# Queueing the vector pieces of the attention values ahead of the gate/value vector work of the next matmul group

## The chip, the cores and the metric

One NeuronCore of a Trainium2 chip. The metric is the device time of one execution in microseconds (us), the median over runs. Engines are named as in the profile: PE is TensorE's matmuls, PEld its weight loads, DVE is VectorE, ACT is ScalarE, POOL is GpSimd, SP is SyncE. L320 is line 320 of the kernel.

## The reference

Attention with a local window of 96 keys and 8 global keys, on 4 batches of 8 heads, 768 positions and head size 64, feeds a gated feed-forward block:

```python
scores = scale * q @ k.T + bias(head, distance); masked outside window and global keys
a = softmax(scores);  x = (a @ v) as [3072 tokens, 512]
out = (silu(x @ w_gate) * (x @ w_val)) @ w_out      # w: 512 x 1536, 1536 x 512
```

## The kernel before

It interleaves two streams by hand. One is the feed-forward stream: for each of 8 token blocks of 384 tokens and 12 slices of 128 hidden units a gate group, a value group and an output group of matmuls. The other is a list of attention steps (`tr` transposes, `sc` scores, `va` values), of which one is put in whenever enough matmul work has gone by. The order of calls is the order on each engine: in the trace of this kernel a transpose of `den` whose input was complete at 43.78 us starts at 45.88, after the `sl` of 45.41 that was called before it.

An attention value block leaves TensorE as a numerator `num` and a denominator `den` in two PSUM banks. Its vector work is not issued at once but appended to a list:

```python
            def invert():                       # PSUM den -> 1/den, one number per 32 columns
                nc.vector.transpose(dT[:, 0:n_q], den[:, 0:n_q])
                nc.vector.reciprocal(out=dR[:, 0:nb], in_=...dT...)

            def spread():                       # back to 128x384
                nc.vector.transpose(rb..., dR...)
                if not fast:
                    nc.gpsimd.tensor_mul(dst, ns[:, 0:n_q], rb[:, 0:n_q])   # L279, dst is in xT

            def scale_num():                    # batch 0 only
                nc.vector.tensor_mul(dst, num[:, 0:n_q], rb[:, 0:n_q])      # L282

            later.append(invert)
            later.append(spread)
            if fast:
                later.append(scale_num)
            else:
                nc.scalar.copy(out=ns[:, 0:n_q], in_=num[:, 0:n_q])
```

The gate and value groups:

```python
        products(t, f, which, c0, NC)                     # 4 matmuls into one of 3 or 4 rotating PSUM banks
        if which == 0:
            nc.scalar.activation(out=th, in_=dst, func=AF.Tanh, scale=0.5)
            nc.vector.scalar_tensor_tensor(out=sl, in0=th, ..., in1=dst, ...)   # L320, frees the bank
        else:
            nc.vector.tensor_mul(hTs[t][:, f, :], dst, gv["sl"])                # L324, frees the bank
```

The scores step multiplies the exponentials by a mask, on VectorE or on GpSimd (L234, L238): both inputs are in SBUF. And the loop:

```python
    for t, f, work, fn in groups:
        ...                              # loads of later batches; at f == 0 all pieces are popped
        fn()                             # a gate, value or output group
        run_later(1)                     # one pending piece
        owed += work * quota.get(t, 0.0)
        while owed >= 1.0 and todo:
            run_later(len(later))
            for step in todo[0][1].pop(0):
                step()
            ...
```

The loads that matter below are issued from GpSimd's queue in this order, ahead of the loop: `load_w(3)`, `load_wo(0)`, `load_wo(1)`, `load_wo(2)`, `load_qk(1, 2, 4)` (queries and keys of batch 1, heads 2 and 3), `load_v_rest(1, 0..3)`; `load_qk(1, 4, 8)` follows in the loop.

The softmax here doesn't subtract the row's maximum and nothing guards it: scores larger than these inputs give would overflow.

Of the kernel before, what the change touches and what calls it, by code (L numbers as in the profile page):

```python
# [37 lines left out]
def kernel(  # L38
# [137 lines left out]
    def run_later(n):  # L176
        for _ in range(n):
            if later:
                later.pop(0)()
# [291 lines left out]
    for t, f, work, fn in groups:  # L471
        if (t, f) not in seen:
            seen.add((t, f))
            for ld in loads.get(NFF * t + f, []):
                ld()
        if f == 0:
            run_later(len(later))
        if t == 1 and f == 0:
            state["x"] = ["x0", "x1", "x2"]
        fn()  # L480
        run_later(1)
        owed += work * quota.get(t, 0.0)
        while owed >= 1.0 and todo:
            run_later(len(later))
            for step in todo[0][1].pop(0):
                step()
            owed -= 1.0
            if not todo[0][1]:
                assert t <= todo[0][0]
                todo.pop(0)  # L490
                owed = 0.4
# [39 lines left out]
```

## Time and profile before

| | before |
|---|---|
| time, median of 4 runs | 270.75 us (270.39 to 271.23) |
| span in the profile | 268.5 us |
| TensorE busy | 247.8 us, 92% |
| VectorE busy | 181.3 us, 68%, 389 instructions |
| TensorE's waits after 43 us | 4.0 us in all |

How to read it: an engine's busy share says little by itself; TensorE's busy share is high nearly everywhere, so what VectorE does matters only where TensorE stops for it. The prediction below shows the lines: the stretches, TensorE's own waits, and the two places in the timeline where those waits lie.

All mask products of VectorE in the kernel before (durations are min/median/max in ns, then the time of the first and last start).

```profile
L238 DVE TENSOR_TENSOR at<-at,masks x52: 341/380/2980, 10.1 to 197.3; 128x432 f16<-128x432 f16 x52
```

The median is 380 ns, the longest 2980.

### The profile page before, as it was taken

How to read it: one execution, taken by the hardware profiler on the slowest of the kernel's cores; microseconds unless marked ns; L12 is line 12 of the kernel's file. 1: busy time of each engine (PE TensorE's matmuls, PEld its weight loads, DVE VectorE, ACT ScalarE, POOL GpSimd, SP SyncE). 2: the span in 40 equal slices, each digit the busy share in tenths (PEclk: the TensorE clock that was granted, in tenths of full speed). 3: DMA queues.
4: the chain of work that ended last, by engine and by line, in shares of the span. 5: the costliest groups of instructions: out<-in, count | busy, mean ns of one | idle time of the engine just before them, and what ended most of it. 6: DMA issues, size and time to landing. Idle time of an engine off the chain costs nothing.

```text
span 268.5 us, 5705 instructions
## 1 busy us (share of the span) xinstructions
PE 247.8 (92%) x2240; PEld 142.2 (53%) x2240; DVE 181.3 (68%) x389; ACT 141.0 (53%) x297; POOL 113.0 (42%) x130
## 2 busy tenths in 40 slices
PE   1787899899999999999979999999999999999993
PEld 1463455456556655555546555565566555555541
DVE  2588798886787677766797496666667755555610
ACT  4568635777566566655553755664663333323321
POOL 8985552268987237464482244413342200000000
PEclk9999999999999999999999999999999999999999
DMA  8999999945996100977345201100100010001011
GB/s 105 167 170 193 195 205 205 177 46 37 212 166 45 44 39 2 157 103 92 57 60 37 49 1 42 39 4 39 42 38 4 39 43 39 7 32 42 39 78 78
DMA packets 45529, 21.27 MB, mean 79 GB/s; under 512 B 28256, under 2 KB 42432, under 8 KB 45504
## 3 DMA queue, kind: packets, MB, share of 16 engines
q0 software_dynamic: 41504, 14.20, 46.6%
q1 hardware_dynamic: 4000, 6.72, 6.8%
q8 instruction: 17, 0.28, 0.4%
q14 instruction: 8, 0.07, 0.1%
HBM read 28.58 MB, written 6.29 MB: 130 GB/s over the span
## 4 chain that ended last, share of the span: by engine, by line
PE 74%; DVE 14%; ACT 7%; issue 2%; DMA 2%; POOL 0%; DVEq 0%; ACTq 0%; POOLq 0%
PE ops L334 22%; PE vps L307 20%; PE gps L307 19%; PE den L256 4%; PE scA L221 3%; ACT at L227 3%; PE num L256 3%; DVE sl L320 3%; DVE at L238 2%; DVE hT L324 2%; DMA kst<-in_k_dram 2%; DVE kT L204 1%; DVE rb L275 1%; DVE dT L269 1%; DVE xT L282 1%
## 5 line engine op out<-in xcount | busy, mean ns | idle before, releaser
L318 ACT ACTIVATE th<-gps 128x384 f32<-128x384 f32 x96 | 47.9, 499 | 66.7 <-PE gps L307 64.2
L307 PE MATMUL gps<-xT,wg 128*128 128x384 f16 x384 | 78.8, 326 | 2.1 <-DVE hT L324 1.3
L307 PE MATMUL vps<-xT,wv 128*128 128x384 f16 x384 | 78.7, 326 | 0.9 <-DVE sl L320 0.9
L320 DVE SCALAR_TENSOR_TENSOR sl<-th,gps 128x384 f32<-128x384 f32 x96 | 52.2, 544 | 39.9 <-ACT th L318 39.8
L334 PE MATMUL ops<-wo,hT 128*128 128x512 f16 x288 | 76.0, 379 | 0.6 <-ACT osb L339 0.6
L324 DVE TENSOR_TENSOR hT<-vps,sl 128x384 f16<-128x384 f32 x96 | 52.7, 549 | 11.6 <-PE vps L307 4.3
L307 PEld LDWEIGHTS <-wg 128*128 128x128 f16 x384 | 36.1, 98 | 34.0 <-issue 3.0
L279 POOL TENSOR_TENSOR xT<-ns,rb 128x384 f16<-128x384 f32 x24 | 23.9, 997 | 68.3 <-DVE rb L275 65.5
L307 PEld LDWEIGHTS <-wv 128*128 128x128 f16 x384 | 36.1, 98 | 26.8 <-issue 3.6
L334 PEld LDWEIGHTS <-hT 128*128 128x128 f16 x288 | 27.1, 98 | 25.3 <-issue 1.2
L227 ACT ACTIVATE at<-scA 128x432 f16<-128x432 f32 x48 | 25.8, 537 | 16.2 <-PE scB L221 16.2
L238 DVE TENSOR_TENSOR at<-at,masks 128x432 f16<-128x432 f16 x52 | 28.1, 566 | 2.1 <-ACT at L227 1.7
L234 POOL TENSOR_TENSOR at<-at,masks 128x432 f16<-128x432 f16 x24 | 24.3, 1034 | 12.2 <-ACT at L227 12.0
L227 ACT ACTIVATE at<-scB 128x432 f16<-128x432 f32 x48 | 26.1, 543 | 0.0
L339 ACT ACTIVATE osb<-ops 128x512 f32<-128x512 f32 x24 | 14.4, 602 | 19.0 <-PE ops L334 18.9
L123 POOL DMA_DIRECT2D vS<-in_v_dram x24 | 21.5, 900 | 3.9 <-DMA wo<-in_moe_w_out_dram 1.6
L256 PE MATMUL den<-at,ones 128*64 128x216 f16 (+6 forms) x288 | 17.8, 237 | 2.0 <-DVE at L238 1.0
L290 ACT COPY ns<-num 128x384 f32<-128x384 f32 x24 | 11.5, 478 | 15.1 <-PE num L256 13.2
L275 DVE STREAM_TRANSPOSE rb<-dR 128x384 f32<-128x384 f32 x32 | 18.3, 573 | 1.3
L269 DVE STREAM_TRANSPOSE dT<-den 128x384 f32<-128x384 f32 x32 | 18.3, 570 | 0.3 <-PE den L256 0.3
L256 PEld LDWEIGHTS <-ones 128*64 128x64 f16 x288 | 11.9, 112 | 11.7 <-issue 9.8
L221 PE MATMUL scA<-qT,kT 64*128 64x216 f16 (+2 forms) x112 | 15.0, 255 | 3.2 <-DVE kT L208 2.4
(32 smaller groups left out, 182.6 us busy)
## 6 DMA issues: line engine op xcount, KB each, us to landing
out_dram<-osb SPq DMA_DIRECT2D x24, 256.0 KB, 2.0
vS<-in_v_dram POOLq DMA_DIRECT2D x20, 120.0 KB, 4.6
qst<-in_q_dram POOLq DMA_DIRECT2D x5, 384.0 KB, 5.8
kst<-in_k_dram POOLq DMA_DIRECT2D x5, 384.0 KB, 7.8
wg<-in_moe_w_gate_dram POOLq DMA_DIRECT2D x4, 384.0 KB, 8.9
wv<-in_moe_w_val_dram POOLq DMA_DIRECT2D x4, 384.0 KB, 10.1
wo<-in_moe_w_out_dram POOLq DMA_DIRECT2D x3, 512.0 KB, 14.1
qst<-in_q_dram POOLq DMA_DIRECT2D x6, 192.0 KB, 6.2
```

Source lines behind the costliest of these rows:

```text
L123: nc.gpsimd.dma_start(out=vSs[b][NG:NG + n, c, :, :], in_=v[b, :, KC * c:KC * c + n, :].rearrange("h p d -> p h d"))
L221: nc.tensor.matmul(sc[hi][:, col:col + n], lhsT=self.kT[r, 128 * c:128 * c + 128], rhs=self.qT[r, q0:q0 + n], start=True, stop=True)
L227: nc.scalar.activation(out=at, in_=sc[hi][:, 0:BANK], func=AF.Exp, scale=scale)
L234: mul_eng.tensor_mul(a2, a2, m[:, WIN:2 * WIN].unsqueeze(1).broadcast_to([128, 2, WIN]))
L238: mul_eng.tensor_mul(at, at, m[:, o:o + BANK])
L256: nc.tensor.matmul(dst[r, o:o + n], lhsT=ones if ones_side else vSs[b][:, c, 2 * hp + hi, :], rhs=self.at[hi, cb][:, col:col + n], start=( ...
L279: nc.gpsimd.tensor_mul(dst, ns[:, 0:n_q], rb[:, 0:n_q])
L307: nc.tensor.matmul(gv[f, which][:, 0:TB], lhsT=w[:, c, 128 * f:128 * f + 128], rhs=xT[:, c, TB * t:TB * t + TB], start=(c == 0), stop=(c = ...
L318: nc.scalar.activation(out=th, in_=dst[:, 0:TB], func=AF.Tanh, scale=0.5)
L320: nc.vector.scalar_tensor_tensor(out=sl, in0=th, scalar=1.0, in1=dst[:, 0:TB], op0=AluOp.add, op1=AluOp.mult)
L324: nc.vector.tensor_mul(hTs[t][:, f, :], dst[:, 0:TB], gv["sl"])
L334: nc.tensor.matmul(ops, lhsT=hTs[t][:, f, 128 * i:128 * i + 128], rhs=wo[:, f, :], start=(f == 0), stop=(f == NFF - 1))
```

## The change

Its intent: a value block's pieces should run in VectorE's idle time while TensorE and ScalarE are still at the next group's gate product, instead of behind the vector instruction that waits for them.

```diff
             state["x"] = ["x0", "x1", "x2"]
+        run_later(1)
         fn()
-        run_later(1)
         owed += work * quota.get(t, 0.0)
```

## The prediction

> **What bounds the kernel now.** I read the page first, then the table of stretches, then TensorE's own waits, and only then the timeline where those waits lie.
>
> ```profile
> span 268.5 us, 5705 instructions
> ...
> PE 247.8 (92%) x2240; PEld 142.2 (53%) x2240; DVE 181.3 (68%) x389; ACT 141.0 (53%) x297; POOL 113.0 (42%) x130
> ...
> L320 DVE SCALAR_TENSOR_TENSOR sl<-th,gps 128x384 f32<-128x384 f32 x96 | 52.2, 544 | 39.9 <-ACT th L318 39.8
> ...
> L275 DVE STREAM_TRANSPOSE rb<-dR 128x384 f32<-128x384 f32 x32 | 18.3, 573 | 1.3
> L269 DVE STREAM_TRANSPOSE dT<-den 128x384 f32<-128x384 f32 x32 | 18.3, 570 | 0.3 <-PE den L256 0.3
> ```
>
> TensorE (PE) is busy 92% of the span, VectorE (DVE) 68%. Before its gate product `sl` VectorE sits idle for 39.9 us in all, waiting for ScalarE's `th`, while the attention pieces queued behind that product (transpose `dT`, reciprocal `dR`, transpose back `rb`) could have run: that idle time is the intent of the change. But VectorE's idle time is worth something only where TensorE waits for VectorE. The stretches (TensorE busy is the first number after the length):
>
> ```profile
> 24.00:51.00 27.00, 23.08 (x258) 13.12 (x258) 23.68 (x57) 15.47 (x37) 11.23 (x15) 1.00 1.50 194
> 60.00:78.00 18.00, 18.00 (x174) 10.40 (x171) 13.08 (x30) 11.77 (x26) 15.17 (x18) 1.00 1.08 133
> 125.00:142.00 17.00, 15.34 (x129) 8.59 (x129) 14.19 (x24) 8.72 (x19) 9.66 (x10) 1.00 0.45 55
> 142.00:200.00 58.00, 57.23 (x541) 32.61 (x537) 39.39 (x85) 34.10 (x73) 20.48 (x21) 1.00 0.14 29
> ```
>
> Outside the first 51 us TensorE is saturated nearly everywhere (18.00 of 18.00, 57.23 of 58), except from 125 to 142 us, where 1.66 us are lost. TensorE's waits from 43 us to the end, the ones that can matter here:
>
> ```profile
> PE gps L307 <- DVE hT L324: 1.3, 1, 1.3
> PE vps L307 <- DVE sl L320: 0.9, 3, 0.4
> PE trq L193 <- DVE xT L282: 0.7, 1, 0.7
> ...
> PE scA L221 <- DVE xT L282: 0.3, 1, 0.3
> ```
>
> All of TensorE's waits after 43 us sum to 4.0 us (these 3.2, and 0.8 for ScalarE). That is the ceiling: 4.0 of 268.5 is 1.5%, so a gain over 2% is not in reach even if every one went. Two places hold most of it. First, the stretch where the vector engine is the path (32 to 51 us, the last of batch 0's values):
>
> ```profile
> 34.29 0.70 POOL L112 DMA_DIRECT2D kst<-in_k_dram  x1 [0.26 <-DMA qst<-in_q_dram]
> 45.41 0.56 DVE L320 SCALAR_TENSOR_TENSOR sl<-th,gps 128x384 f32<-128x384 f32 x1 [0.94 <-ACT th L318]
> 48.35 0.53 PE L193 MATMUL trq<-ident,qst 128*64 128x128 f16 x12 [0.71 <-DVE xT L282]
> 48.69 0.53 PE L193 MATMUL trk<-ident,kst 128*64 128x128 f16 x12
> 50.97 0.26 PE L221 MATMUL scA<-qT,kT 64*128 64x216 f16 x1 [0.34 <-DVE xT L282]
> ```
>
> Each row has start, length, and in brackets the idle time before it and who ended it. Second, a collision of VectorE with GpSimd (POOL):
>
> ```profile
> 130.63 0.55 DVE L320 SCALAR_TENSOR_TENSOR sl<-th,gps 128x384 f32<-128x384 f32 x1 [1.36 <-ACT th L318]
> 132.27 0.56 DVE L275 STREAM_TRANSPOSE rb<-dR 128x384 f32<-128x384 f32 x1
> 132.98 0.99 POOL L279 TENSOR_TENSOR xT<-ns,rb 128x384 f16<-128x384 f32 x1 [2.76 <-ACT at L227]
> 133.20 3.92 DVE L238 TENSOR_TENSOR at<-at,masks 128x432 f16<-128x432 f16 x2
> 137.64 0.81 PE L307 MATMUL gps<-xT,wg 128*128 128x384 f16 x4 [1.30 <-DVE hT L324]
> ```
>
> Two mask products of VectorE, which take 0.67 us together where GpSimd is quiet (as at 60.74 us), take 3.92 us here; VectorE falls behind, the gate/value banks are not freed, and TensorE stands 1.30 us, and 0.36 us more at 140.76.
>
> [...] the transpose at 45.88 us has its `den` complete since about 43.8 us and starts only after the `sl` of 45.41. [...] the mask product (both inputs in SBUF) takes 0.37 us alone and 1.0 to 1.2, once 2.98 us, beside a GpSimd product, while `sl` and `hT` (one input in PSUM) stay at 0.54 and 0.55 us. [...] the trace has 570 for `dT`, and I use the trace.
>
> **The change part by part.** It removes and adds no instruction: 389 VectorE instructions before and after. In the loop of gate, value and output groups one pending piece is now popped ahead of the group instead of behind it. Twenty-eight of the 32 value blocks are handled in that loop (4 of batch 0's second halves, 24 of batches 1 to 3). Each gives an inversion (570 + 228 = 0.80 us), a spreading (0.57 us), and in batch 0 a scaling on VectorE (0.56 us) or else a product on GpSimd (1.0 us) that the spreading releases. So a piece moves one VectorE instruction earlier: inversion, `sl`, spreading, `hT` where it was `sl`, inversion, `hT`, spreading. The inversion can't be held up by what it now precedes, for `den` is computed on TensorE before the group's matmuls. So 0.80 us of each block moves into an idle stretch where there is one. Where VectorE has no idle time the sum stays.
>
> *Stage 1.* From 32 to 44 us VectorE is almost without a gap, so reordering gives little there (about 0.1 us per dependent pair that now has another instruction between). At 44.4 us comes the idle 0.94 us. The inversion (0.80) now fits in it, so the scaling that ends at 48.21 should end near 47.4, and the last one, at 50.91, near 50.1. TensorE's last value matmul before the transposes ends at 47.64: the 0.71 us wait for `xT` is gone. But what follows needs batch 1's keys. That transfer was issued at 34.29 us and its time to landing in the list of DMA issues is 14.2 us: it lands at 48.5. So the `trk` transposes, which began at 48.69, can begin only 0.2 us earlier. After them the scores at 50.97 lose their 0.34 us wait, since the last scaling is then 0.8 us earlier. Sum: 0.2 + 0.34, less some issue time: 0.5 us. The rest of the expected 1.0 us is turned into a wait for keys.
>
> *Stage 2.* At 130.63 the inversion now runs in the idle 1.36 us ahead of `sl`. The spreading follows `sl` directly: it ends near 131.18 + 0.5 = 131.7 instead of 132.83, GpSimd's `xT` product then runs from about 131.8 to 132.8[...]. Both should be done by about 133.8, before GpSimd's own mask products can start (134.3). Then VectorE is not behind and the 1.30 + 0.36 = 1.66 us of TensorE waits go. The margin is only 0.2 us, so I give it a weight of 0.7: 1.2 us.
>
> *Elsewhere* TensorE waits for ScalarE (0.40 of the 0.9 at 92.44 us, behind the key copies; 0.6 for `osb`) or not at all. Moving VectorE's pieces changes nothing there. The sum is 0.5 + 1.2 = 1.7 us; 271.07 - 1.7 = 269.4 us.
>
> **The rivals.** (a) *TensorE is the bound, nothing comes through*: for it, the saturated stretches; against it, the two places above. It would give 271. (b) *The transfer takes all of stage 1 and the collision stays*, only displaced: GpSimd's work is released earlier, and what it then meets depends on tenths of a microsecond; other mask products at 54, 78, 100, 112 and 158 us are also stretched (1.5 to 2.1 us a pair) without stalling TensorE. This gives 270.5 to 271. (c) *The piece in front holds up the gate/value work*: `sl` or `hT` comes 0.6 to 0.8 us later where VectorE has no gap, its bank is freed later and TensorE stalls. For it, VectorE is 23.68 of 27 us busy in stage 1; against it, three or four banks rotate, so TensorE can be some three products of 0.65 us ahead, and in the two-block steps the backlog (`sl` at 99.42 starts 0.9 us after its `th`) shrinks. If it bites in a few places: 271.5 to 272.5. (d) *Stage 1 isn't capped by the keys*, and all four `xT` waits of that stretch (0.65 at 37.83, 0.32 at 42.24, 0.71, 0.34) go, 2.0 us, with stage 2: 267.4. The landing time at 48.5 speaks against it.
>
> **Range and chances.** The main path gives 269.4; without stage 2, 270.6; with all of both, 268.9; a spread of 0.3 us between runs comes on top. So 268.4 to 270.9 for 8 in 10. Faster by 2% needs 265.6 or less, 5.4 us, more than TensorE's waits: 1%. Slower by 2% needs 5.4 us of new stalls, a string of new collisions: 1%. Within 2%: 98%.
>
> **What would show it right or wrong.** Right: 389 VectorE instructions; the inversion's `dT` ahead of `sl` after each value block; idle time before `sl` well under 39.9 us; TensorE's waits for `xT` after 43 us gone, with a wait for the keys (`trk`, until about 48.5 us) in their place; scores near 50.5 instead of 50.97; the pair of mask products near 133 us under 1.2 us and no 1.3 us stall of `gps` after it; VectorE's busy time some 2 us lower for fewer collisions. Wrong: a new long mask product elsewhere with TensorE waiting behind it, more time in `gps` or `vps` waiting for `hT` or `sl`, or the keys landing at another time.

Cut from it, and marked, is what no trace or run of this case shows. In *Stage 2*, "both" are VectorE's two mask products; the cut clause had the first of them, whose input is ready at 132.98 us, start clear of GpSimd's product, which was to end at 132.8. The 0.1 us per dependent pair in *Stage 1* is an estimate: in the kernel before, `dR` starts 0.04 us after `dT` ends (46.49 and 46.45), while `dT`, which does not need the `sl` ahead of it, starts 0.09 us before that ends (45.88 and 45.97).

## The result, and the profile after

The changed kernel took 268.69 us in the median (268.47 to 268.96, 4 runs) against 270.75: ratio 0.9923, interval 0.9902 to 0.9945. A ratio here is the mean time of one kernel's fast runs over that of the other's of the same rounds, so it is not quite the ratio of the medians. Executions over 1.5% slower than the fastest of the same kernel are left out of the means. The prediction had 269.4, with 268.4 to 270.9 as its range. The gain of 0.8% is clear of the noise.

The page of the changed kernel, TensorE's and VectorE's share and the gate product's row:

```profile
PE 247.8 (93%) x2240; PEld 142.0 (53%) x2240; DVE 174.8 (66%) x389; ACT 140.9 (53%) x297; POOL 112.1 (42%) x130
...
L320 DVE SCALAR_TENSOR_TENSOR sl<-th,gps 128x384 f32<-128x384 f32 x96 | 52.6, 548 | 42.9 <-ACT th L318 42.3
```

389 VectorE instructions as before, but 6.5 us less busy. The idle time before `sl`, the very thing that the change was to fill, rose from 39.9 to 42.9 us: VectorE, less held up elsewhere, waits for `th` more often. The mask products explain the lower busy time:

```profile
L238 DVE TENSOR_TENSOR at<-at,masks x52: 360/376/1190, 10.4 to 195.6; 128x432 f16<-128x432 f16 x52
```

Their sum went from 28.1 to 20.4 us on the page, the longest from 2980 to 1190 ns. That is 7.7 us of VectorE time, of which only a small part reached the end of the kernel. The stretches say where:

```profile
24.00:51.00 27.00, 24.84 (x268) 14.06 (x270) 23.94 (x60) 15.79 (x37) 11.18 (x15) 0.94 1.50 194
125.00:142.00 17.00, 16.84 (x156) 9.67 (x155) 11.71 (x27) 9.62 (x21) 9.56 (x11) 1.00 0.45 55
```

From 125 to 142 us TensorE is now busy 16.84 us instead of 15.34. (The first stretch is not to be compared by its busy time: its granted clock, the number after POOL's, was 0.94 in this run, so its matmuls took longer.) The place near 133 us after the change:

```profile
131.17 0.57 DVE L275 STREAM_TRANSPOSE rb<-dR 128x384 f32<-128x384 f32 x1
...
131.89 0.99 POOL L279 TENSOR_TENSOR xT<-ns,rb 128x384 f16<-128x384 f32 x1 [2.76 <-DVE rb L275]
...
133.11 0.76 DVE L238 TENSOR_TENSOR at<-at,masks 128x432 f16<-128x432 f16 x2
...
136.33 0.82 PE L307 MATMUL gps<-xT,wg 128*128 128x384 f16 x4
```

The transpose back follows `sl` (130.69) directly, GpSimd's product is over at 132.88, and the pair of mask products takes 0.76 us instead of 3.92. The gate group that had waited 1.30 us follows the matmul before it, and starts at 136.33 instead of 137.64. TensorE's waits after 43 us:

```profile
PE vps L307 <- DVE sl L320: 0.7, 3, 0.4
PE ops L334 <- ACT osb L339: 0.6, 1, 0.6
PE trq L193 <- DVE dR L270: 0.5, 1, 0.5
PE trk L193 <- DMA kst<-in_k_dram: 0.4, 1, 0.4
```

The waits for `xT` are gone, and a wait for the keys has taken their place. At that place:

```profile
48.14 0.53 PE L193 MATMUL trq<-ident,qst 128*64 128x128 f16 x12 [0.46 <-DVE dR L270]
...
49.03 0.53 PE L193 MATMUL trk<-ident,kst 128*64 128x128 f16 x12 [0.36 <-DMA kst<-in_k_dram]
...
50.89 0.26 PE L221 MATMUL scA<-qT,kT 64*128 64x216 f16 x1
```

The scores begin 0.08 us earlier than before (50.89 against 50.97), not 0.5. They are not free to: they come 1.91 us after the keys' landing at 48.98 us. The wait of `trq` is put down to `dR`, but the weight load of that transpose started 0.04 us after the landing of the queries at 48.09 us: it is a wait for that load.

Following the same matmul in both traces, the lead of the changed kernel is 0.07 us at 51 us, none at 125, 1.3 at 137.6, 1.5 at 140.8, and 1.8 from 157.6 us to the end. (This trace had come into the first stage late: its granted clock was 0.50 from 24 to 26 us and 0.74 from 26 to 28, and at 33 us it was 0.72 us behind the kernel before. By 42 us it had made up 0.69 of that.) So one more small place, at 157.6 us, was not in the prediction. There, in the kernel before:

```profile
156.97 0.57 DVE L269 STREAM_TRANSPOSE dT<-den 128x384 f32<-128x384 f32 x1
...
157.31 0.25 PE L221 MATMUL scA<-qT,kT 64*128 64x216 f16 x1
...
157.59 0.25 PE L221 MATMUL scB<-qT,kT 64*128 64x216 f16 x1
```

The second scores matmul starts at 157.59 us, when `dT` has ended (157.54), 0.28 us after its partner; elsewhere the two start together. It waits for the bank of `den`, which the inversion frees. No list of waits shows it: a matmul's record lasts 0.25 us though the next one normally starts 0.1 us later, so only 0.03 us looks idle.

### The profile page after: what moved, and what is told of

It is laid out like the page before. It is cut to its first block, busy times and chain, and to the rows that moved or that the text cites. A ratio compares the mean times of both kernels' runs of the same rounds, so it can differ in the third digit from the quotient of the medians.

```text
span 266.7 us, 5704 instructions
## 1 busy us (share of the span) xinstructions
PE 247.8 (93%) x2240; PEld 142.0 (53%) x2240; DVE 174.8 (66%) x389; ACT 140.9 (53%) x297; POOL 112.1 (42%) x130
## 4 chain that ended last, share of the span: by engine, by line
PE 74%; DMA 12%; POOL 5%; ACT 5%; issue 2%; DVE 1%; ACTq 0%; POOLq 0%
PE ops L334 23%; PE vps L307 21%; PE gps L307 19%; DMA kst<-in_k_dram 8%; DMA wv<-in_moe_w_val_dram 4%; PE den L256 3%; PE num L256 3%; PE scA L221 3%; ACT at L227 2%; POOL vS L117 1%; PE trq L193 1%; POOL qst L112 1%; PE trk L193 1%; ACT kT L204 1%; ACT osb L339 1%
## 5 line engine op out<-in xcount | busy, mean ns | idle before, releaser
L320 DVE SCALAR_TENSOR_TENSOR sl<-th,gps 128x384 f32<-128x384 f32 x96 | 52.6, 548 | 42.9 <-ACT th L318 42.3
L234 POOL TENSOR_TENSOR at<-at,masks 128x432 f16<-128x432 f16 x24 | 23.7, 1010 | 15.7 <-ACT at L227 10.3
L238 DVE TENSOR_TENSOR at<-at,masks 128x432 f16<-128x432 f16 x52 | 20.4, 413 | 3.8 <-ACT at L227 3.3
```

The source lines that it names most:

```text
L234: mul_eng.tensor_mul(a2, a2, m[:, WIN:2 * WIN].unsqueeze(1).broadcast_to([128, 2, WIN]))
L238: mul_eng.tensor_mul(at, at, m[:, o:o + BANK])
L320: nc.vector.scalar_tensor_tensor(out=sl, in0=th, scalar=1.0, in1=dst[:, 0:TB], op0=AluOp.add, op1=AluOp.mult)
```

## The experiments

Three theories. *Two places*: the gain is that of the place near 133 us (1.66 us), the first stage's is capped by the keys' landing. *Many small gains*: it is spread over all 28 value blocks. *Backlog*: near 133 us VectorE is simply late, and it is not GpSimd's work that matters. All twelve kernels gave correct results. "Before" below is the kernel before in the same rounds: 271.10 us for the first four runs, 270.94 for the next four, 270.90 for the last four.

**1. The changed kernel once more.** No edit.

> The changed kernel once more, beside the others on this chip. 268.7 us, 2.0 us under the kernel before (ratio 0.992). All theories expect this; it is the measure for the parts.

268.96 us (267.76 to 270.57), ratio 0.9929. As expected in the mean; two of the six runs are near 270.4, which becomes of interest below.

**2. Pieces ahead in the first token block alone.**

```diff
-        fn()
-        run_later(1)
+        ahead = bool(later) and t == 0
+        if ahead:
+            run_later(1)
+        fn()
+        if not ahead:
+            run_later(1)
```

> Pieces ahead only in the first token block (four value blocks of batch 0), behind elsewhere. Theory of two places: 0.4 us faster than before (270.3), the scores after the last batch 0 value block about 0.4 us earlier, and the long mask product near 133 us still there with its 1.3 us stall. Rival (many small gains over all 28 value blocks): 4 of 28 parts of 2.0 us, 0.3 us, so time alone does not tell these two apart; a rival in which the vector-bound first stage is the whole gain expects 2.0 us.

271.24 us (270.37 to 273.0), ratio 1.0018 (0.9986 to 1.0050): no gain, where 0.4 us was expected. The profiled run is one of the two slowest (273.0), and shows how the first stage can lose. Up to 42 us it leads by 0.6 us; then it waits for the queries (which land at 49.4 here) and the keys (50.3). The stretches of this run; the granted clock is the third number from the right:

```profile
47.00:49.00 2.00, 0.03 (x1) 0.00 (x0) 1.97 (x6) 0.00 (x0) 0.33 (x1) 1.00 1.79 174
49.00:51.00 2.00, 1.47 (x24) 1.22 (x24) 0.30 (x1) 0.70 (x1) 0.43 (x1) 0.54 2.32 157
51.00:53.00 2.00, 2.00 (x14) 0.93 (x8) 0.18 (x1) 1.29 (x4) 0.00 (x0) 0.61 1.60 192
```

After a wait of 2.37 us the granted clock was 0.54 and 0.61 in these 4 us, and the four matmuls of the gate product at 51.17 us started 0.32 us apart instead of 0.16 (as at 45.56). So in this trace TensorE arrived early at a late transfer and then ran at a lower clock; that the wait is what lowered it is the author's reading of this one trace. That the other slow runs of this kernel, and the two of run 1, have the same cause is not shown, for they were not profiled.

**3. Pieces ahead in all later token blocks.** The same edit with `t > 0`.

> Pieces behind in the first token block, ahead in all later ones (24 value blocks). Theory of two places: 1.66 us faster than before (269.1), all of it where the mask products near 133 us no longer collide. First-stage rival: 0 us.

269.15 us (268.45 to 269.77), ratio 0.9927, equal to the whole change (0.9929) within the noise. The first stage's part is nil on this chip; the rest is 0.7% or 2.0 us. The pair of mask products takes 0.76 us.

**4. The pieces of one value block ahead.** The same loop with `later[0].ahead`, and where the pieces are made:

```diff
+            invert.ahead = (b, hp, half) == (2, 3, 0)
+            spread.ahead = (b, hp, half) == (2, 3, 0)
+            scale_num.ahead = False
             later.append(invert)
             later.append(spread)
```

> Only the two pieces of one value block (batch 2, last head pair, first half), the one just before the long mask product, go ahead; the other 27 blocks stay behind. Theory of two places: this alone gives 1.66 us (269.1), as much as moving all 24 later blocks. Rival (many small gains): one 28th of 2.0 us, under 0.1 us, so 270.7.

269.51 us (269.09 to 269.72), ratio 0.9941: 0.59% of 271 is 1.6 us, from one block of 28. This refutes the many small gains. What is left to run 3 is 0.4 us by the ratios (their intervals overlap); the traces put 0.28 of it at 157.6 us, where run 3 gained it and run 4 did not. The pair near 133 us took 0.76 us in this run too.

**5. Inversions ahead, spreadings behind.** As in run 4, with `invert.ahead = True`, `spread.ahead = False` for all blocks.

> Inversions ahead of the group, spreadings behind as before, in all blocks. Collision theory: GpSimd's product near 133 us is released by the spreading, which now ends near 132.3 instead of 131.7 us (the inversion has moved out of its way but hT still precedes it), so the product runs about 132.3 to 133.3 us and still meets the first mask product at 133.1; the first one stretches, the second may escape: between 0.4 and 2.0 us faster than before, 269.8 if part of the stall stays. Rival (it is the inversion in idle time that gains, wherever the spreading is): full gain, 268.7.

268.73 us (268.23 to 268.95), ratio 0.9918: the whole gain, as the rival said. The collision theory had 269.8 for it. GpSimd's product ran from 132.76 to 133.76, beside the first mask product, and yet:

```profile
132.76 1.00 POOL L279 TENSOR_TENSOR xT<-ns,rb 128x384 f16<-128x384 f32 x1 [2.75 <-DVE rb L275]
...
133.33 0.97 DVE L238 TENSOR_TENSOR at<-at,masks 128x432 f16<-128x432 f16 x2
133.71 0.96 POOL L123 DMA_DIRECT2D vS<-in_v_dram  x1
...
134.69 1.97 POOL L238 TENSOR_TENSOR at<-at,masks 128x432 f16<-128x432 f16 x2
```

GpSimd works without a gap here, product, load issue, two mask products, as it did before the change; VectorE's pair lost 0.3 us, not 3.2. So that GpSimd's product meets the first mask product is not what costs.

**6. One product on VectorE, old order.**

```diff
-        return lambda: pairs[b, hp].values(half, b == 0)
+        return lambda: pairs[b, hp].values(half, b == 0 or (b, hp, half) == (2, 3, 0))
```

> The kernel before with its old order; only for the one value block before 133 us the final product runs on VectorE instead of GpSimd, so VectorE has 0.56 us more work there and GpSimd 1.0 us less. Collision theory: nothing of GpSimd meets the first mask product; the 1.3 us stall goes, 1.0 to 1.66 us faster (269.1 to 269.8). Rival (VectorE is simply late there, its backlog makes the stall): 0.56 us more backlog, so as slow or slower, 270.7 to 271.3.

271.10 us (270.54 to 274.46), ratio 1.0026: no gain. But the test is confounded. The pair of mask products took 0.67 us and the wait of `gps` was gone, as the collision theory has it; in its place, the scores ahead of it waited:

```profile
133.62 0.26 PE L221 MATMUL scA<-qT,kT 64*128 64x216 f16 x1 [1.17 <-DVE xT L282]
```

Without ScalarE's copy, the bank of `num` is held until VectorE's product, and the scores need that bank. TensorE lost 1.3 us there and won it back by 137.7 us, where the kernel before has its stall. Its time decides nothing.

**7. Keys earlier, old order.** `load_qk(1, 2, 4)` ahead of the output weights:

```diff
     load_w(3)
+    load_qk(1, 2, 4)
     load_wo(0)
     load_wo(1)
     load_wo(2)
-    load_qk(1, 2, 4)
```

> The kernel before with batch 1's second query and key load issued ahead of the three output-weight loads, so that they land near 40 us instead of 48. Keys-cap theory: nothing to gain here, for the transposes wait for xT until 48.2 us anyway: within 0.2 us of before. If the keys were a bound in the kernel before too: up to 0.4 us faster.

270.51 us (270.10 to 270.68), ratio 0.9984 (0.9968 to 0.9999). The keys landed at 41.1 instead of 48.5 us, and that was worth about 0.4 us (0.0 to 0.9 by the interval), more than the 0.2 that the theory allowed. In the profiled run the scores of this stage began at 51.03 us, no earlier than the 50.97 of the kernel before.

**8. Keys earlier, changed order.** The same edit of the changed kernel.

> The changed kernel with the same earlier load of queries and keys. Keys-cap theory: the waits of trq and trk for the load near 48 us go, and the gain of the first stage that they had taken comes out: 0.5 to 0.9 us faster than the changed kernel, 267.8 to 268.2. Rival (first stage has nothing more to give): 268.7.

268.24 us (267.65 to 268.45), ratio 0.9899. Against 0.9929 in run 1 (on another chip) that is 0.8 us. In the traces, this kernel leads the changed one by 1.8 us at 49 us, and by only 0.5 us after 56 us (0.9 of the 1.8 was there at 33 us already, for the changed kernel's trace had begun this stage late): at 55.91 the next transposes waited 1.16 us for the second load of keys (`load_qk(1, 4, 8)`, landing at 55.87). The gain had run into the next transfer.

**9. GpSimd's product twice.** The changed kernel with

```diff
                     nc.gpsimd.tensor_mul(dst, ns[:, 0:n_q], rb[:, 0:n_q])
+                    if (b, hp, half) == (2, 3, 0):
+                        nc.gpsimd.tensor_mul(spare, ns[:, 0:n_q], rb[:, 0:n_q])
```

> The changed kernel; for the one value block ahead of 133 us GpSimd computes its product twice, the second time into a spare tile, so that GpSimd is in a product of SBUF operands when VectorE's mask products start. VectorE's order and backlog are those of the changed kernel. Collision theory: the pair of mask products takes 3 us or more again, gps waits 1 us or more for hT, and the time rises by 1.0 to 1.7 us over the changed kernel (269.7 to 270.4). Rival (VectorE's late start was the cause): unchanged, 268.7.

268.95 us (268.40 to 271.31), ratio 0.9945 (0.9915 to 0.9974). The stall did not come back; the collision theory in the form that predicted it has failed a second time:

```profile
132.84 1.00 POOL L282 TENSOR_TENSOR spare<-ns,rb 128x384 f16<-128x384 f32 x1
133.11 1.26 DVE L239 TENSOR_TENSOR at<-at,masks 128x432 f16<-128x432 f16 x2
133.78 0.96 POOL L123 DMA_DIRECT2D vS<-in_v_dram  x1
```

(The edit shifts the line numbers.) The first mask product took 0.97 us and ended 0.24 us after the second GpSimd product (134.08 and 133.84); the second took 0.37 us, beside the load issue, and was through at 134.37.

**10. The load issue between them moved, old order.**

```diff
-            loads[base + step * (2 + c)] = [lambda b=b, c=c: load_v_rest(b, c)]
+            at_group = 42 if (b, c) == (3, 2) else base + step * (2 + c)
+            loads.setdefault(at_group, []).append(lambda b=b, c=c: load_v_rest(b, c))
```

> The kernel before, old order; only the issue of one value load (batch 3, third chunk), which GpSimd ran between its attention product and its two mask products near 134 us, is moved two blocks later. If GpSimd working without a gap (product, load issue, product, product) is what kept the second mask product out for 2.98 us: it gets in at 134.0, the pair takes 1.2 to 1.5 us, the 1.3 us stall goes and the time falls by 1.0 to 1.7 us (269.2). If a product alone beside it is enough: no change, 270.9.

269.31 us (268.98 to 269.99), ratio 0.9949 (0.9934 to 0.9965): 1.4 us of the gain without touching VectorE's order. But the edit caught another issue than the text says: it moved the one that had run at 129.27 us, which now joins the one at 133.93, so that two of them, not none, stand between GpSimd's product and its mask products.

```profile
132.91 1.31 DVE L238 TENSOR_TENSOR at<-at,masks 128x432 f16<-128x432 f16 x2
133.63 1.84 POOL L123 DMA_DIRECT2D vS<-in_v_dram  x2
```

The first mask product took 1.02 us beside the product, as in the kernel before; the second took 0.37 us. So backlog is refuted as the cause: VectorE has its old order and is as late as before (first mask product 0.22 us after GpSimd's product began, as in the kernel before), and TensorE's wait of 1.30 us is gone.

**11. Both loads of batch 1's queries and keys early, changed order.**

```diff
     load_w(3)
+    load_qk(1, 2, 4)
     load_wo(0)
-    load_wo(1)
-    load_wo(2)
-    load_qk(1, 2, 4)
     for c in range(4):
         load_v_rest(1, c)
+    load_qk(1, 4, 8)
+    load_wo(1)
+    load_wo(2)
 ...
-    loads = {10: [lambda: load_qk(1, 4, 8)]}
+    loads = {}
```

> The changed kernel with both remaining query and key loads of batch 1 ahead of the second and third output-weight loads. In the run with only the first of them ahead, the gain of 1.8 us at 49 us shrank to 0.5 us at a wait for the second key load near 55 us. Keys-cap theory: with that one early as well the gain stays, 1.0 to 1.8 us faster than the changed kernel (266.9 to 267.7). Rival (another load takes its place[...]): 268.2 or slower.

267.08 us (266.85 to 267.21), ratio 0.9861 (0.9846 to 0.9876): the best of all, 1.4% under the kernel before, and with the narrowest range. TensorE has no wait for a load after 24 us.

**12. The same loads, old order in the first token block.** The edit of run 11 on the kernel of run 3.

> The same loads, with the pieces of the first token block behind their group as in the kernel before and ahead in all later ones. Keys-cap theory: with the keys out of the way the order in the first block is worth what it was predicted to be without the cap, 0.8 to 1.3 us, so this is that much slower than the run before it. Rival (the order in the first block is worth nothing): equal to it.

268.69 us (268.53 to 269.18), ratio 0.9924 (0.9910 to 0.9939). The order in the first block is worth 0.9924 - 0.9861 = 0.63%, 1.7 us, once the keys are out of the way, a little more than expected. The scores that end this stage, first here, then in run 11:

```profile
50.96 0.26 PE L221 MATMUL scA<-qT,kT 64*128 64x216 f16 x1 [0.35 <-DVE xT L282]
```

```profile
49.51 0.26 PE L221 MATMUL scA<-qT,kT 64*128 64x216 f16 x1
```

1.45 us apart, with the keys landed at 41.6 us in run 12 and 40.8 in run 11; the wait of the scores for `xT` is gone in run 11 alone. Runs 2, 3 and 12 together: the same reorder gives nothing with the keys late and 1.7 us with the keys early.

## Why the prediction was right, and where it was off

*The bound.* Right: TensorE is busy all but a few us, VectorE's idle time is worth nothing by itself, and a gain over 2% was out of reach. VectorE became 6.5 us less busy and the kernel 2.1 us shorter.

*Stage 2, 1.66 us with a weight of 0.7.* The effect came whole: GpSimd's product was foreseen from about 131.8 to 132.8 and ran from 131.89 to 132.88; the pair of mask products was foreseen to be done by about 133.8 and was at 133.87; one block alone gave 1.6 us. The weight was the error of size: 1.2 in the sum, 1.6 measured. One reading in it was wrong without harm: 134.3 us, when GpSimd's own mask products "can start", is when the input of the second is complete. That of the first is complete at 133.81 us before the change, and after it that product started at 134.03, 0.16 us after VectorE's pair was done.

Its cause was named too coarsely. Prediction and first theory had the first mask product clear of GpSimd's product. Runs 5 and 9 have the first mask product beside a GpSimd product and lose 0.3 and 0.6 us of VectorE's time, with no wait of TensorE behind it. What costs is the 2.98 us of the second one. It came in three traces with the old order (the kernel before, and runs 2 and 7). In the kernel before, beside the pair of 133.20 us:

```profile
133.26 0.55 ACT L227 ACTIVATE at<-scA 128x432 f16<-128x432 f32 x1
...
134.90 1.97 POOL L238 TENSOR_TENSOR at<-at,masks 128x432 f16<-128x432 f16 x2
```

There the second mask product began 0.33 us after the input of GpSimd's own first mask product was complete (134.14 and 133.81), and that product was the next behind the load issue under way; VectorE's ended at 137.12, after both GpSimd products (134.90 to 136.87). In runs 2 and 7 the pair took the same 3.92 us, at 135.48 and 133.49. In run 5 the second one began 0.17 us before that input, in run 9 0.13 us after it, in run 10 0.32 us after it but with a second load issue in between; each time it took 0.37 us. That a mask product of GpSimd that is ready and next behind a load issue goes ahead of one of VectorE is the author's reading; it fits these four traces if 0.13 us is too short for it, and was not shown. Another meeting cost less: at 79.05 us in the kernel before, VectorE's mask product began while one GpSimd product ran and the next one's input was complete, and it took 1.18 us and was through before that next one. No run varied the interval alone, so the reason stays open.

*Stage 1, 0.2 + 0.34, less some: 0.5 us.* This term was wrong: runs 2 and 3 put it at nothing within the noise. Its mechanism was right, VectorE's pieces did come earlier (`dT` at 44.48 instead of 45.88 us) and the keys took the gain. What failed is the step "it lands at 48.5" used as a fixed time. The keys of this load landed at 48.5 us in the kernel before, but between 48.6 and 50.3 in the nine other traces with that order of loads; 0.5 us later and there is nothing left. The cap shows directly: in six traces (the changed kernel and runs 1, 4, 5, 9, 10; 4 and 10 with the old order in this stage) the scores began 1.90 to 1.91 us after that landing, whenever it was; in the other four it was 2.2 to 2.9 us, with a later `xT` or, in run 2, the low clock. In run 2 the longer wait (2.37 us) was followed by a granted clock of 0.54 and 0.61. A step before that was wrong too, "reordering gives little there" of the time from 32 to 44 us. Between 36 and 42 us the changed order gained 0.67 to 0.69 us on the old one in each pair of traces that can be compared (the changed kernel, runs 2 and 8 against the kernel before, run 11 against run 12): TensorE's waits for `xT` of 0.65 and 0.32 us became one of 0.31. Rival (d), which had all of the `xT` waits go for 2.0 us, is what run 11 against run 12 then showed, 1.7 us, with the keys moved.

*Elsewhere nothing.* Not quite: 0.28 us at 157.6 us, a wait that the list of idle times can't show.

*Its marks.* Right: 389 instructions, no `xT` waits, a wait for the keys instead, the pair under 1.2 us. Wrong: the idle time before `sl`, expected well under 39.9 us, rose to 42.9; the scores of the first stage came at 50.89, not 50.5; VectorE's busy time fell by 6.5 us, not 2. Rival (c), that pieces in front hold up `sl` or `hT`, did not show: TensorE's waits for those two fell from 2.2 to 0.7 us.

So it was partly luck that the 269.4 was near 268.69: the terms were off in opposite directions, -0.5 in the first stage, +0.4 and +0.3 in the others. The prediction also counted from 271.07 us for the kernel before, which measured 270.75 beside the changed kernel; that is 0.3 of the 0.7 us between them. The gain was forecast as 1.7 us and measured as 2.1.

## What to carry to other kernels

When a queue's order is changed, ask at each place where the bounding engine stops, not at how much idle time is filled: here 28 blocks were moved and one of them made 1.6 us of some 2.0. And before counting a removed wait, look at what would be waited for next, with its spread from run to run: here a transfer that landed at 48.5 to 50.3 us took the gain of the first stage, and with it moved (run 11 against run 12, keys landed at 40.8 and 41.6) the reorder of that stage was worth 1.7 us.
